# The first batch's steps in a fixed order, without T·B·K, merges by pairs of heads, the first weight split beside the substitution

## The chip, the cores and the metric

The kernel runs on one core of a Trainium2 chip. The metric is device time in microseconds (us), the median over runs. The engines of a core work side by side, each through its own list of instructions in order: PE (TensorE, matmuls; weight loads are listed as PEld), DVE (VectorE), ACT (ScalarE), POOL (GpSimd) and SP (SyncE, which here only issues DMAs). TensorE's clock has two levels, 1.2 and 2.4 GHz, which the profile gives as a granted share of 0.5 or 1.

## The reference

Two blocks: a delta-rule recurrence per head, then a Fourier mix with an MLP.

```python
B, H, S, D = 4, 8, 768, 48
k_n = k / (norm(k) + 1e-6);  state = zeros(B, H, D, D)
for t in range(S):
    y[:, :, t] = q_t @ state                       # before the update
    v_old = state.T @ k_t
    state += b_t * outer(k_t, v_t - v_old)
x = y.transpose(0, 2, 1, 3).reshape(B, S, 384)
u = x + real(fft(fft(x, axis=1), axis=2))
un = (u - mean(u)) / sqrt(var(u) + 1e-6)           # over the last axis
out = u + relu(un @ w_ch1) @ w_ch2                 # 384 -> 1536 -> 384
```

The two weights arrive as float64 and are turned into float32 on the chip, by integer work on their two 32-bit words.

## The kernel before, in words

**Chunks and quads.** The recurrence is worked in chunks of 64 tokens: 12 per batch, 48 in all, m = 0 to 47. Four chunks are a *quad* (three per batch, Q = 0 to 11), two quads a *group* g. For each quad `prepare` (L337) transposes keys and queries (`pt`, into KQT), takes their products (`pg`) and copies them out: key by key into A (L400 on DVE, L402 on ACT), query by key, masked, into LQ (L405, DVE). In the first batch keys and queries are prepared apart.

**Inverse.** Each chunk and head needs the inverse T of a 64x64 triangular matrix. `invert` (L428) turns the gram matrices so that each lane of DVE holds one (transpose L441), takes the key norms from the diagonal (`sm`), and does 30 steps of substitution (L465, L467) for blocks of 32x32, then turns the result back into Z and A (L483, L484). Groups 0 and 1 are inverted together. `merge` (L489) joins two 32-blocks to one 64-block by two rounds of small products (`pj`) and writes the table `wt`. A *round* is one of these two, for one quad.

**The chain.** `chain(m)` (L541) has three pieces, each the end of a `yield`: U = V − K·state (`pc<-st,KQT`, DVE L572); then for batches 1 to 3 U = T·U by `wt` (`pc<-U,wt`, ACT L584); then state += K·U (`pc<-U,kp`, DVE L600). In the first batch `combined` (L521) instead multiplies T into keys (`pm`) and values (`pv`) two chunks ahead, with two ACT copies, so that the chain itself is without the second piece. `outputs` (L610) forms y for two chunks (`py`), by an ACT copy (L635) and a DVE addition (L640, L642) into the x tiles.

**Second block.** `fourier(b)` (L668) mixes batch b (adds on DVE and POOL, products `pf` and `pb`), then means and variances; `mlp` (L755) takes three groups of 256 rows (`ph` with the first weight, `po` with the second). `weights(0)` converts w_ch1 (two ACT instructions L302, L304 and three DVE instructions L321, L324, L327 for a piece of 384 columns, 12 pieces), `weights(1)` w_ch2.

**What sets the order.** The body (L870 on) writes instructions as generators advance: in each piece of a chain step, `due` grows by PRE for preparation, inversion and merge of the next group and by SIDE for the second block of the batch before. The Tile framework then orders the instructions of each engine by its own planning, except where `keep_in_program_order` binds one. Batch 0 runs beside w_ch1's conversion; `second(0)` runs beside batch 1, and so on; the last batch's second block comes after all chains.

Of the kernel before, what the change touches and what calls it, by code (L numbers as in the profile page):

```python
# [10 lines left out]
F32 = mybir.dt.float32  # L11
# [6 lines left out]
CH = 64  # L18
W = 32
# [63 lines left out]
def kernel(  # L83
# [56 lines left out]
    nc.vector.memset(k0[:, D:], 0.0)  # L140
# [11 lines left out]
    kps = [zeroed([128, QT, 4, 64], f"kp{i}", nc.vector, pads) for i in range(NB)]  # L152
    qps = [zeroed([128, QT, 4, 64], f"qp{i}", nc.vector, pads) for i in range(1)]
# [61 lines left out]
    half_p = const.tile([NBH, 1], F32, name="half_p")  # L215
    nc.gpsimd.memset(half_p, 0.5)
    half_n = const.tile([128, GT], F32, name="half_n")
    nc.gpsimd.memset(half_n, -0.5)
    root = const.tile([NBH, 1], F32, name="root")
    nc.scalar.activation(root, half_p, ACT.Sqrt)  # L220

    bblk = const.tile([128, B * NQ * QT * 4], F32, name="bblk")

    def betas():
# [8 lines left out]
        nc.vector.tensor_copy(bcol.rearrange("p (b i) (c u) -> p b (i c) u", b=B, u=4),  # L233
# [4 lines left out]
        nc.vector.tensor_scalar(twice, twice, once, None, op0=ALU.mult)  # L238
        nc.vector.transpose(bblk, bcol.rearrange("p q n -> p (q n)"))
# [23 lines left out]
    def weights(part):  # L263

        if moe_w_ch1.dtype == F32:
            if part == 0:
                nc.sync.dma_start(out=w1, in_=moe_w_ch1.rearrange("(c p) f -> p c f", p=128))
            else:  # L270
                yield
                nc.sync.dma_start(out=w2, in_=moe_w_ch2.rearrange("(c p) m -> p c m", p=128))
            return
        w1v = moe_w_ch1.bitcast(I32).rearrange("(c p) (f two) -> p c f two", p=128, two=2)
        w2v = moe_w_ch2.bitcast(I32).rearrange("(c p) (m two) -> p c m two", p=128, two=2)
        nw = DFF // 2
        np_ = nw // 2
        if part == 0:
            halves = [(w1v[:, i, a * nw:a * nw + nw], w1[:, i, a * nw:a * nw + nw])
                      for i in range(KD) for a in range(2)]  # L280
            n, stage = 2, wk.tile([128, 2, nw, 2], I32, tag="hT", name="w64")
            stages = [stage[:, i] for i in range(2)]
        else:
            halves = [(w2v[:, i, a * np_:a * np_ + np_], w2[:, i, a * np_:a * np_ + np_])
                      for i in range(KF) for a in range(DM // np_)]
            n, stages = 1, [xpairs[6].rearrange("p t (f two) -> p (t f) two", two=2).bitcast(I32)]

        def fetched(i):
            if i < len(halves):
                nc.sync.dma_start(out=stages[i % 2], in_=halves[i][0])  # L290

        def words(p):
            t, cs = stages[p // n % 2], slice(p % n * np_, (p % n + 1) * np_)
            return t[:, cs, 0], t[:, cs, 1], tmps[:, p % 2]

        def first(p):

            lo, hi, t = words(p)
            tc.keep_in_program_order(nc.scalar.activation(  # L302
                t[:, 0], lo.bitcast(mybir.dt.uint32), ACT.Copy, scale=2.0 ** -29))
            tc.keep_in_program_order(nc.scalar.activation(  # L304
                t[:, 1].bitcast(F32), hi.bitcast(F32), ACT.Abs, scale=2.0 ** -112))

        for i in range(len(stages)):
            fetched(i)
        yield
        if part == 1:  # L310
            stages.append(wk.tile([128, np_, 2], I32, tag="scr", name="w64"))
            fetched(1)
        tmps = wk.tile([128, 2, 2, np_], I32, tag="F", name="wtmp")
        first(0)
        for p in range(n * len(halves)):
            lo, hi, t = words(p)
            dst = halves[p // n][1][:, p % n * np_:(p % n + 1) * np_].bitcast(I32)
            low, mag = t[:, 0], t[:, 1]
            if p + 1 < n * len(halves):
                first(p + 1)  # L320
            tc.keep_in_program_order(nc.vector.scalar_tensor_tensor(  # L321
                low, hi, -2 ** 31, low, op0=ALU.bitwise_and, op1=ALU.bitwise_or))
            yield
            tc.keep_in_program_order(nc.vector.tensor_scalar(  # L324
                mag, mag, 3, None, op0=ALU.logical_shift_left))
            u16 = mybir.dt.uint16
            nc.vector._custom_dve(dve_ops.ADD32_U16LIMBS, out=dst.bitcast(u16),  # L327
                                  in0=mag.bitcast(u16), in1=low.bitcast(u16))
            if (p + 1) % n == 0:
                fetched(p // n + 2)  # L330
            yield
# [3 lines left out]
    grams = {}  # L335

    def prepare(Q, parts=(0, 1)):  # L337
# [6 lines left out]
        if 0 in parts:  # L344
            if lh == 0:

                if g == 1:
                    grams[g] = w2.rearrange("p c m -> p (c m)")[:, 0:2 * QT * 4 * 2 * W].rearrange(
                        "p (c u l s) -> p c u l s", c=2 * QT, u=4, l=2)
                else:  # L350
                    grams[g] = wk.tile([128, 2 * QT, 4, 2, W], F32, tag="A", name="A")
# [6 lines left out]
        for c2 in range(QT // 2):  # L358
            for c in (2 * c2, 2 * c2 + 1):
# [8 lines left out]
                if QT * i + c < NCH // 2 or 1 not in parts:  # L368
                    nc.scalar.activation(dst, src, ACT.Copy)  # L369
                else:  # L370

                    if na == 2:
                        nc.scalar.activation(dst[:, 0], src[:, 0], ACT.Copy)
                    nc.scalar.activation(dst[:, na - 1], src[:, na - 1, :, ::-1], ACT.Copy)
# [568 lines left out]
```

## Time and profile before

| | us |
|---|---|
| median of 3 runs (806.78 to 818.7) | 809.28 |
| the profiled execution | 807.02 |
| its span, first to last instruction | 805.3 |
| busy in the span: PE / DVE / ACT / POOL | 691.7 / 382.3 / 263.0 / 55.5 |

The profiled execution is 1.7 us longer than its span. Busy time says how much of the span an engine was at work; in which stretch and behind which wait it stood still has to be read from the views below. "x16" beside a matmul counts instructions: a product of two float32 tiles is two of them, so eight products stand as x16.

### The profile page before, as it was taken

To read this page: it belongs to the slowest core of one execution; us is meant where nothing else is said; L and a number is where in the kernel's file an instruction comes from. 1 tells how busy PE (TensorE), PEld (TensorE's weight loads), DVE (VectorE), ACT (ScalarE), POOL (GpSimd) and SP (SyncE) were. 2 spreads that over 40 slices of the span, in tenths; PEclk is the share of its full clock that TensorE was granted. 3 is DMA by queue.
4 is the path that set the end of the run, shared out by engine and by line. 5 is a ranking of instruction groups with operands and counts; after the bars stand their busy time and mean duration, and the time that the engine had idled before them with its cause. 6 is when DMAs were issued, how large, how long until landed. Compare 5 with 4: busy or idle time off the path is not lost.

```text
span 805.3 us, 19785 instructions
## 1 busy us (share of the span) xinstructions
PE 691.7 (86%) x8600; PEld 513.8 (64%) x8600; DVE 382.3 (47%) x968; ACT 263.0 (33%) x622; POOL 55.5 (7%) x73
## 2 busy tenths in 40 slices
PE   5810798866999989689999999899999989999997
PEld 4600686665757757577575775676767657587684
DVE  3899536577991166835792113986111135200000
ACT  3400775621627422273123443223311122021120
POOL 5020000010000010001100000210000010000000
PEclk9999999867899995799999999899999999999999
DMA  6620046330431121101201100101000000000000
GB/s 107 179 55 0 2 117 140 66 57 25 137 94 32 21 50 37 31 8 23 43 16 25 41 13 12 31 2 30 13 11 11 11 11 1 11 11 20 11 10 21
DMA packets 82232, 30.89 MB, mean 38 GB/s; under 512 B 77296, under 2 KB 78832, under 8 KB 82144
## 3 DMA queue, kind: packets, MB, share of 16 engines
q1 hardware_dynamic: 78800, 26.24, 14.5%
q0 software_dynamic: 1168, 2.98, 1.2%
q8 instruction: 68, 1.11, 0.6%
q10 hardware_dynamic: 2176, 0.39, 0.3%
q14 instruction: 20, 0.16, 0.1%
HBM read 24.87 MB, written 4.72 MB: 37 GB/s over the span
## 4 chain that ended last, share of the span: by engine, by line
PE 64%; DVE 19%; ACT 7%; DMA 4%; issue 3%; SPq 2%; POOL 1%; POOLq 0%; ACTq 0%; DVEq 0%
PE ph L124 20%; PE po L124 19%; PE pc L124 5%; DVE A L465 4%; PE pg L124 3%; PE pf L124 3%; PE pj L124 3%; PE py L124 3%; PE pt L127 3%; ACT A L402 2%; DVE w L467 2%; DVE X L467 2%; DMA w<-in_moe_w_ch_dram 2%; PE pb L124 2%; SPq L169 2%
## 5 line engine op out<-in xcount | busy, mean ns | idle before, releaser
L124 PE MATMUL ph<-unT,w 128*128 128x256 f32 x864 | 213.2, 395 | 3.9 <-ACT hT L781 2.4
L124 PE MATMUL po<-w,hT 128*128 128x384 f32 x576 | 200.4, 495 | 0.9 <-ACT hT L781 0.4
L124 PEld LDWEIGHTS ph<-unT,w 128*128 128x128 f32 x864 | 160.5, 194 | 32.2 <-ACT hT L781 5.4
L124 PEld LDWEIGHTS po<-w,hT 128*128 128x128 f32 x576 | 104.9, 190 | 66.6 <-ACT hT L781 1.0
L781 ACT ACTIVATE hT<-ph 128x256 f32<-128x256 f32 x144 | 55.1, 384 | 179.2 <-PE ph L124 179.0
L794 DVE TENSOR_TENSOR x<-x,po 128x384 f32<-128x384 f32 x24 | 13.2, 549 | 103.5 <-PE po L124 103.5
L124 PE MATMUL pj<-Z,A 32*32 32x32 f32 x640 | 13.2, 201 | 45.5 <-DVE Z L483 45.2
L600 DVE TENSOR_TENSOR st<-st,pc 128x192 f32<-128x192 f32 x44 | 15.5, 351 | 68.5 <-PE pc L124 54.1
L465 DVE TENSOR_TENSOR A<-X 128x30 f32<-128x30 f32 (+14 forms) x120 | 42.8, 357 | 2.3
L402 ACT ACTIVATE A<-pg 32x256 f32<-32x256 f32 x104 | 35.7, 371 | 23.9 <-PE pg L124 23.3
L124 PE MATMUL pg<-KQT 48*64 48x64 f32 (+1 forms) x1024 | 38.8, 297 | 5.3 <-ACT KQT L369 4.5
L124 PEld LDWEIGHTS pj<-Z,A 32*32 32x32 f32 x640 | 12.2, 116 | 48.6 <-issue 43.6
L467 DVE TENSOR_TENSOR X<-X,A 128x30 f32<-128x30 f32 (+14 forms) x120 | 40.5, 337 | 2.3
L124 PE MATMUL pf<-stab,scr 128*128 128x128 f32 (+6 forms) x192 | 30.9, 310 | 12.1 <-DVE scr L692 11.9
L124 PEld LDWEIGHTS pg<-KQT 48*64 48x64 f32 x1024 | 31.0, 172 | 15.5 <-ACT KQT L369 6.9
L124 PE MATMUL py<-st,KQT 48*64 48x48 f32 x768 | 32.7, 246 | 8.3 <-DVE x L642 7.4
L572 DVE TENSOR_TENSOR U<-V,pc 128x192 f32<-128x192 f32 x48 | 16.8, 350 | 47.8 <-PE pc L124 46.2
L584 ACT ACTIVATE U<-pc 128x192 f32<-128x192 f32 x36 | 12.0, 332 | 83.5 <-PE pc L124 64.2
L661 POOL DMA_INDIRECT out_dram<-x,rows_hi x12 | 12.4, 1033 | 364.1 <-DVE x L794 174.6
L124 PEld LDWEIGHTS pf<-stab,scr 128*128 128x128 f32 (+2 forms) x192 | 26.9, 198 | 16.3 <-issue 7.3
L405 DVE TENSOR_TENSOR LQ<-pg,pack 128x512 f32<-128x512 f32 x24 | 16.4, 683 | 43.2 <-ACT A L402 39.4
L718 DVE TENSOR_TENSOR x<-x,pb 128x193 f32<-128x193 f32 (+1 forms) x96 | 26.4, 347 | 18.8 <-PE pb L124 18.8
(137 smaller groups left out, 908.8 us busy)
## 6 DMA issues: line engine op xcount, KB each, us to landing
qp<-in_q_dram SPq DMA_DIRECT2D x96, 48.0 KB, 2.4
V<-in_v_dram SPq DMA_DIRECT2D x96, 48.0 KB, 2.5
w<-in_moe_w_ch_dram SPq DMA_DIRECT2D x6, 768.0 KB, 6.0
kp<-in_k_dram SPq DMA_DIRECT2D x80, 48.0 KB, 2.5
x<-in_moe_w_ch_dram SPq DMA_DIRECT2D x6, 384.0 KB, 3.1
w<-in_moe_w_ch_dram SPq DMA_DIRECT2D x6, 384.0 KB, 3.4
out_dram<-x SPq DMA_DIRECT2D x8, 192.0 KB, 1.9
out_dram<-x SPq DMA_DIRECT2D x4, 168.0 KB, 2.1
```

What stands on the lines that cost most here:

```text
L124: return nc.tensor.matmul(o, lhsT=lhsT, rhs=rhs, start=start, stop=stop, skip_group_check=True)
L127: nc.tensor.matmul(o, lhsT=src, rhs=ident[0:src.shape[0], 0:src.shape[0]], is_transpose=True, start=start, stop=True, skip_group_check=True)
L169: engs[hh].dma_start(out=dst[64 * hh:64 * hh + CH, c, :, 0:D], in_=src[b, 4 * hh:4 * hh + 4, t0:t0 + CH, :].rearrange("h p d -> p h d"))
L402: nc.scalar.activation(ce(A[pr, ns, :, sl]), src, ACT.Copy)
L405: nc.vector.tensor_tensor(ce(LQ[:, 2 * c2:2 * c2 + 2]), pv[:, :, :, 1 - a0], mb[:, None, None, :].broadcast_to([128, 2, 4, CH]), op=ALU.mult)
L465: nc.vector.tensor_tensor(t, X[:, :, j:j + 1, j + 1:].broadcast_to([128, G, j, n]), X[:, :, 0:j, j:j + 1].broadcast_to([128, G, j, n]), op ...
L467: nc.vector.tensor_tensor(X[:, :, 0:j, j + 1:], X[:, :, 0:j, j + 1:], t, op=ALU.add)
L572: nc.vector.tensor_tensor(U.rearrange(ue, e=2), V4[:, c].rearrange(ue, e=2), pk, op=ALU.subtract)
L600: nc.vector.tensor_tensor(nst, st, pS, op=ALU.add)
L718: nc.vector.tensor_tensor(dst, dst, src, op=op)
L781: nc.scalar.activation(hT[:, fc, :], ph, ACT.Relu)
L794: nc.vector.tensor_tensor(x[g][:, tt, :], x[g][:, tt, :], po, op=ALU.add)
```

## The change

1. The first batch's chain gets the second piece too (T·U by `wt`); `combined` goes.
2. `merge` takes the 32-blocks of two heads at once: 64x64 products of which the two diagonal blocks are kept, half as many matmuls; the copies out are four of half the size instead of two. A is stored with its two copies apart, `[2, chunk, head, s]`.
3. Gram copies: two over 128 lanes and two over 32, instead of six over 32; in the first batch on ACT for the first half of a quad and on DVE for the second. The first batch's LQ is copied by ACT without its mask, and DVE masks it in SBUF later.
4. All four first quads' queries are prepared during the substitution (two before). w_ch1 is fetched in ten pieces of 384 KB from POOL's queue and split in place by ACT during the substitution; DVE joins it during the first batch.
5. From the end of the first substitution to the end of the first batch every DVE, ACT and PE instruction keeps program order, with a table that says what goes beside which piece of a step. Only quad 0 is merged before the chain starts; the second group's last transposes, the merges of quads 1 to 3 and the join go between the steps.
6. Preparation of group 2 (quads 4 and 5) starts with the second batch (PRE 4.6 there), not in the middle of the first. SIDE is 0, 1.5, 2.2, 2.2 for batches 0 to 3 (2.4 before).

```diff
+    class Ordered:
...
+        def __getattr__(self, name):
+            def call(*args, **kwargs):
+                ins = getattr(self.engine, name)(*args, **kwargs)
+                if strict[0]:
+                    tc.keep_in_program_order(ins)
+                return ins
+            return call
+
+    dve, act, pe = Ordered(nc.vector), Ordered(nc.scalar), Ordered(nc.tensor)
...
+    class FirstWeight:
+        def fetch(self, p, eng=nc.sync):
+            if p < self.n:
+                i, a = divmod(p, DFF // PW)
+                eng.dma_start(out=self.stage(p), in_=moe_w_ch1.bitcast(I32).rearrange(
+                    "(c p) (f two) -> p c f two", p=128, two=2)[:, i, PW * a:PW * a + PW])
+        def split(self, p):
+            if p < self.n:
+                lo, hi = words(self.stage(p))
+                digits(self.stage(p), lo, hi)
+        def join(self):
+            t = wk.tile([128, 2, PW], I32, tag="scr", name="wtmp")
+            for p in range(self.n):
...
+                for k, op in enumerate(joined(w1[:, i, PW * a:PW * a + PW], lo, hi, t[:, 0], t[:, 1])):
+                    op()
...
+                    yield
...
+    class Merge:
+        def products(self, step, half):
+            A, Z = self.A, self.Z
+            if half == 0:
+                self.pj = ps_pair("pj", "pair")
+            for c in (2 * half, 2 * half + 1):
+                n = QT * self.lh + c
+                for us in (slice(0, 2), slice(2, 4)):
+                    for hh in range(2):
+                        r1, r2 = slice(64 * hh, 64 * hh + W), slice(64 * hh + W, 64 * hh + 64)
+                        ops = (A[r2, 1, n, us], Z[r2, n, us]) if step == 0 else (A[r1, 0, n, us], A[r1, 1, n, us])
+                        o = 128 * c + W * us.start
+                        mm(self.pj[64 * hh:64 * hh + 64, hh, o:o + 64],
+                           *(a.rearrange("p u t -> p (u t)") for a in ops), c == 0 and us.start == 0)
...
     def chain(m):
...
-        if m < NCH:
-            if m + 2 < NCH:
-                combined(m + 2)
-        else:
-            pu = pc[:, 0, 4 * D:8 * D].rearrange("p (u d) -> p u d", u=4)
...
+        pu = pc[:, 0, 4 * D:8 * D].rearrange("p (u d) -> p u d", u=4)
...
+        act.activation(U, pu, ACT.Copy)
+        yield
...
-    PRE, SIDE = 2.4, (2.4, 2.4, 2.4, 2.4)
...
+    between = queries(0, 1, 2, 3)
+    for i in range(W - 2):
+        advance(first)
+        advance(between)
+        if i < 10:
+            w.fetch(i, nc.gpsimd)
+        if 10 <= i < 20:
+            w.split(i - 10)
...
+    strict[0] = True
+    M = Merge(0, 0)
...
+    scaled(0)
+    run(masks(0))
+    scaled(1)
+    run(masks(1))
+    pe_work = {m: (outs, outs, outs) if m % 2 == 0 else (outs, None, None) for m in range(2, NCH)}
+    for m, l, step in ((0, 1, 0), (1, 1, 1), (3, 2, 0), (5, 2, 1), (7, 3, 0), (9, 3, 1)):
+        pe_work[m] = (outs if m > 1 else None, P(l, step, 0), P(l, step, 1))
+    act_work = {0: [T(1, 0)], 1: [T(1, 1)], 2: [Dg(1)], 4: [T(2, 0), Dg(2)], 6: [T(2, 1)], 8: [T(3, 0), Dg(3)], 10: [T(3, 1)]}
+    rest = seq(w.join(), masks(3))
+    for m in range(NCH):
...
+        for i, _ in enumerate(chain(m)):
+            if pe_work[m][i]:
+                pe_work[m][i]()
+            if i == 1:
...
+                    advance(*((first, 1) if m < 3 else (rest, 4)))
+            if i == 2:
+                advance(rest, 1)
+                for op in act_work.get(m, ()):
+                    op()
...
+    strict[0] = False
+    PRE, SIDE = 2.4, (0.0, 1.5, 2.2, 2.2)
+    pre, side, due = ahead(2), iter(()), [0.0, 0.0]
+    for m in range(NCH, STEPS):
...
+                due[0] += 4.6 if g == 1 else PRE
+                due[1] += SIDE[b]
```

What the change moves is seen in the order of instructions on an engine. All instructions that go through the new wrapper carry its line, L131.

**PE, the first two steps of the chain** (`pc` are the chain's products, `pv` and `pm` those of T·V and T·K, `pj` merges). Before:

```order
L124 MATMUL pc<-st_89,KQT 64x48 x8
L124 MATMUL pm<-wt_83,kp_73 64x64 x4
L124 MATMUL pv<-V_318,wt_83 64x48 x6
L124 MATMUL pc<-U,kp_73 64x48 x8
L124 MATMUL pv<-V_318,wt_83 64x48
L124 MATMUL pj<-w_128 32x32 x32
L124 MATMUL pc<-st_90,KQT 64x48 x8
```

Changed:

```order
L131 MATMUL pc<-st_89,KQT 64x48 x8
L131 MATMUL pc<-U,wt_83 64x48 x8
L131 MATMUL pj<-Z,A 64x64 x8
L131 MATMUL pc<-U,kp_73 64x48 x8
L131 MATMUL pj<-Z,A 64x64 x8
L131 MATMUL pc<-st_90,KQT 64x48 x8
```

`pm` and `pv` are gone, `pc<-U,wt` stands in the chain, and a merge of 32 products has become two halves of 8.

**DVE, a step of the first batch** (U and st are the chain's two results; SCALAR_TENSOR_TENSOR, TENSOR_SCALAR and ISA on w and wtmp join w_ch1; x is the output addition). Before:

```order
L572 TENSOR_TENSOR U<-V_318,pc 128x2x2x48
L321 SCALAR_TENSOR_TENSOR wtmp<-w_453,wtmp 128x384
L327 ISA w_127<-wtmp 128x768
L600 TENSOR_TENSOR st_89<-st_91,pc 128x192
L321 SCALAR_TENSOR_TENSOR wtmp<-w_453,wtmp 128x384
L572 TENSOR_TENSOR U<-V_318,pc 128x2x2x48
```

Changed:

```order
L131 TENSOR_TENSOR U<-V_310,pc 128x2x2x48
L131 TENSOR_TENSOR x_145<-x_145,py 128x384
L131 SCALAR_TENSOR_TENSOR wtmp<-w_446 128x384
L131 TENSOR_SCALAR wtmp<-w_446 128x384
L131 ISA w_127<-wtmp 128x768
L131 SCALAR_TENSOR_TENSOR wtmp<-w_446 128x384
L131 TENSOR_TENSOR st_90<-st_89,pc 128x192
```

Four join instructions, and in odd steps an output addition ahead of them, now stand between U and st.

**DVE, the end of the first batch** (X<-A opens the inversion of group 2; scr<-x opens the Fourier mix of batch 0; un<-x opens the MLP). Before:

```order
L600 TENSOR_TENSOR st_91<-st_90,pc 128x192
L572 TENSOR_TENSOR U<-V_1364,pc 128x2x2x48
L441 STREAM_TRANSPOSE X<-A 128x1024
L405 TENSOR_TENSOR LQ<-pg,pack 128x2x4x64
L642 TENSOR_TENSOR x_146<-x_146,py 128x384
L561 COPY st_89<-p_2029 128x192
L682 TENSOR_TENSOR scr<-x_146 128x384
```

Changed, some 65 rows behind the first scr<-x and 20 behind the first un<-x:

```order
L131 TENSOR_TENSOR LQ<-pg,pack 128x2x4x64
L131 TENSOR_TENSOR st_90<-st_89,pc 128x192
L131 TENSOR_TENSOR LQ<-pg,pack 128x2x4x64 x2
L131 STREAM_TRANSPOSE X<-A 128x1024
L131 SCALAR_TENSOR_TENSOR wtmp<-wtmp 128x384
```

The inversion of group 2, which stood ahead of the Fourier mix, now stands behind it, among the joins of w_ch2.

## Rows read from the trace of the kernel before

**Rows 1.** Stretches: us; busy PE, PEld, DVE, ACT, POOL; clock; DMA share; GB/s.

```profile
0.00:84.70 84.70, 30.31 (x480) 22.55 (x480) 67.17 (x138) 17.29 (x44) 15.46 (x25) 1.00 0.36 81
98.30:124.50 26.20, 26.19 (x686) 23.27 (x686) 11.28 (x28) 18.92 (x42) 0.00 (x0) 1.00 0.42 102
201.40:242.80 41.40, 38.67 (x270) 27.67 (x270) 38.84 (x102) 19.18 (x44) 1.51 (x2) 0.94 0.38 113
302.50:336.70 34.20, 28.32 (x415) 22.43 (x408) 23.64 (x67) 7.39 (x19) 2.37 (x3) 0.56 0.19 36
```

**Rows 2.** Timeline, DVE, up to the first step: start, us, engine, line, instruction.

```profile
41.31 0.96 DVE L198 TENSOR_TENSOR V<-V,ln 128x768 f32<-128x768 f32 x1 [0.18 <-DMA qp<-in_q_dram]
...
45.78 0.68 DVE L405 TENSOR_TENSOR LQ<-pg,pack 128x512 f32<-128x512 f32 x1
...
80.44 2.36 DVE L476 TENSOR_TENSOR Y<-Y,w 128x1024 f32<-128x1024 f32 x2
82.71 1.97 DVE L483 STREAM_TRANSPOSE Z<-Y 128x1024 f32<-128x1024 f32 x1
...
98.35 0.35 DVE L572 TENSOR_TENSOR U<-V,pc 128x192 f32<-128x192 f32 x1 [1.19 <-PE pm L124]
```

**Rows 3.** Timeline, the chain's products and copies at three places.

```profile
98.76 0.71 PE L124 MATMUL pc<-U,kp 64*64 64x48 f32 x16
...
231.90 0.67 PE L124 MATMUL pc<-U,wt 64*64 64x48 f32 x16
...
235.27 0.45 PE L124 MATMUL pc<-U,kp 64*64 64x48 f32 x16
...
314.23 0.69 PE L124 MATMUL pc<-st,KQT 48*64 48x48 f32 x16
...
315.57 0.55 DVE L642 TENSOR_TENSOR x<-x,py 128x384 f32<-128x384 f32 x1
315.68 1.09 PE L124 MATMUL pc<-U,wt 64*64 64x48 f32 x16
...
316.86 0.33 ACT L584 ACTIVATE U<-pc 128x192 f32<-128x192 f32 x1 [0.59 <-PE pc L124]
```

**Rows 4.** Timeline, DVE, from the last step of the first batch.

```profile
160.32 0.35 DVE L572 TENSOR_TENSOR U<-V,pc 128x192 f32<-128x192 f32 x1 [0.84 <-PE pc L124]
161.94 1.90 DVE L441 STREAM_TRANSPOSE X<-A 128x1024 f32<-128x1024 f32 x1 [1.26 <-ACT A L402]
...
239.10 1.98 DVE L483 STREAM_TRANSPOSE Z<-Y 128x1024 f32<-128x1024 f32 x1
```

**Rows 5.** Timeline, DVE, around the start of the third batch.

```profile
323.80 0.35 DVE L572 TENSOR_TENSOR U<-V,pc 128x192 f32<-128x192 f32 x1 [0.42 <-PE pc L124]
...
356.62 0.35 DVE L572 TENSOR_TENSOR U<-V,pc 128x192 f32<-128x192 f32 x1 [1.83 <-PE pc L124]
```

**Rows 6.** Timeline, PE: products of 64x64 at four places of the array, and a merge round.

```profile
124.83 0.46 PE L124 MATMUL pm<-wt,kp 64*64 64x64 f32 x16
...
241.13 1.20 PE L124 MATMUL pj<-Z,A 32*32 32x32 f32 x64 [1.10 <-DVE Z L483]
```

**Rows 7.** Stretch 166 to 300, instructions of `pt`: busy PE, PEld, ACT.

```profile
166.00:300.00 134.00, 5.02 (x32) 4.02 (x32) 4.91 (x10) 0.90 0.24 59
```

**Rows 8.** Stretch 161.9 to 190, instructions on tile X (the inversion): busy DVE.

```profile
161.90:190.00 28.10, 7.42 (x16) 0.64 0.24 44
```

**Rows 9.** The same stretch, instructions on `sm` (the norms): busy DVE, ACT, POOL.

```profile
161.90:190.00 28.10, 5.00 (x15) 0.23 (x1) 2.25 (x1) 0.64 0.24 44
```

**Rows 10.** Groups by line: busy us, mean ns, then idle before and its releasers.

```profile
L124 PE MATMUL ph<-unT,w 128*128 128x256 f32 x864 | 213.2, 395 | 3.9 <-ACT hT L781 2.4 <-ACT unT L769 0.6 <-ACT gz L715 0.5
L302 ACT ACTIVATE wtmp<-w 128x384 int32<-128x384 uint32 x18 | 10.0, 554 | 8.5 <-DMA w<-in_moe_w_ch_dram 5.7 <-DVE w L327 1.4 <-DMA kp<-in_k_dram 0.9
```

**Rows 11.** DMA issues: KB each, us to landing; and a timeline row of SP's queue.

```profile
w<-in_moe_w_ch_dram SPq DMA_DIRECT2D x6, 384.0 KB, 3.4
...
19.38 5.93 SPq L169 DMA_DIRECT2D V<-in_v_dram  x8
```

More of the change, by code (lines that the diff above doesn't have):

```diff
@@ L273, in weights, with second_weight @@
+    def second_weight():
+        if moe_w_ch1.dtype == F32:
+            yield
+            nc.sync.dma_start(out=w2, in_=moe_w_ch2.rearrange("(c p) m -> p c m", p=128))
             return
-        w1v = moe_w_ch1.bitcast(I32).rearrange("(c p) (f two) -> p c f two", p=128, two=2)
         w2v = moe_w_ch2.bitcast(I32).rearrange("(c p) (m two) -> p c m two", p=128, two=2)
[L276 to L305, printed above, removed]
@@ L307, in weights @@
-        for i in range(len(stages)):
-            fetched(i)
-        yield
[L310 to L322, printed above, removed]
-            yield
[L324 to L330, printed above, removed]
+        stages = [xpairs[6].rearrange("p t (f two) -> p (t f) two", two=2).bitcast(I32)]
@@ L588, in chain @@
             loads()
-            if Q + 1 < len(quads):
+            if Q + 1 < len(quads) and Q + 1 not in vals:
                 values(Q + 1)
@@ L647, in advancing @@
             gens.pop(0)
-        yield
     def store(b, T, x):
@@ L814, in seq, with kept @@
             yield from gen
+    def kept(gen):
+        while True:
+            strict[0] = True
+            more = advance(gen)
+            strict[0] = False
+            if not more:
+                return
+            yield
     def ahead(g):
@@ L875 @@
     run(keys(2, 3))
-    side = weights(0)
-    advance(side)
+    values(1)
+    w = FirstWeight()
     tables()
     first = invert(0, 1)
-    advance(first, 5)
-    between = queries(0, 1)
+    advance(first, 4)
+    between = queries(0, 1, 2, 3)
[6 more added lines that the diff above has]
+            w.split(i - 10)
+    run(between)
     while not isinstance(grams[0], tuple):
@@ L883 @@
         advance(first)
-        advance(between)
-    run(between, both(merge(0, (0,)), merge(0, (1,), "py")))
-    combined(0)
-    combined(1)
-    pre = seq(first, merge(1), queries(2, 3))
-    due = [0.0, 0.0]
-    for m in range(STEPS):
+    strict[0] = True
+    M = Merge(0, 0)
+    for step in range(2):
+        M.products(step, 0)
+        M.products(step, 1)
+        M.taken(step)
+        M.diagonal(step)
+    scaled(0)
+    run(masks(0))
+    scaled(1)
+    run(masks(1))
+    outs = lambda: advancing(later)
```

357 lines of the change are left out of this document (207 added, 150 removed).

## The prediction

> **What bounds the kernel now.** I read the stretches first, then the timeline of DVE at their borders, then the groups. Four regimes are to be seen.
>
> Up to 84.7 the substitution holds DVE (67.2 busy of 84.7) while PE works 30.3 [rows 1]; this head ends with the first U of the chain at 98.35 [rows 2].
>
> The first batch runs from that U to the one of step 11 at 160.32 [rows 4]: 62.0 for 11 steps, 5.6 each. PE is full up to 124.5 (26.2 of 26.2) [rows 1]. The clock column prints 1.00 for the first of these stretches, but the same eight products take 0.71 at 98.76 and 0.45 at 235.27 [rows 3], and 0.69 in a stretch of mean clock 0.56 [rows 1, 3]. So I take PE to be at 1.2 GHz until about 124.
>
> The passage to the second batch runs until Z of group 2 is turned at 239.10 [rows 4]. DVE is the limit there: Fourier mix, inversion and w_ch2; in its second part DVE is busy 38.8 of 41.4 [rows 1].
>
> From there on PE bounds, with one hole: between 302.5 and 336.7 it is busy 28.3 of 34.2 at mean clock 0.56 [rows 1], and step 24's U at 323.80 is followed by step 25's only at 356.62 [rows 5]. By the counts in the body, 51 advances of the MLP at 2.4 a piece are used up after 21 pieces, in step 19; steps 20 to 23 run without any, and step 24 waits for its inversion.
>
> **The change, term by term**, against the profiled execution (807.0; the median is 2.3 higher).
>
> *Head.* From DVE's path before the first Z go four LQ masks and two scalings of V (0.6 and 0.9 from start to start, from rows of 0.68 and 0.96) and the second half of the Y product (1.1): 5.3 [rows 2]. I take 5.0, since the square root's round trip loses some cover. Then, in fixed order on DVE, come the second transpose (1.8, a start-to-start like Z's 1.97), the two scalings and four masks (4.2), then what opens the chain: two small products with v0, p0 and its copy (2.5, estimated from the 0.35 and 0.7 of like instructions [rows 3]) and the first products to U (0.9): 9.4 from Z's end. Z ended at 84.7, so the new U stands at 79.7 + 9.4 = 89.1, against 98.35: −9. Merging quad 0 (two rounds on PE, 12 ACT copies) fits into these 9.4. The extra queries, the fetches and the splits cost nothing as long as they hide under the substitution, where ACT and POOL are busy 17.3 and 15.5 of 84.7 [rows 1]. The splits are 20 x 0.55 = 11 [rows 10]. Five of them stand ahead of the square root in ACT's order and wait for their 384 KB, 3.4 to land [rows 11]; if the transfers come one behind the other, that is 17 after the first issue at about 12, still before the root at 37. Bounds −4 to −12.
>
> *First batch.* A step is now three pieces in line. At 1.2 GHz: 0.69 + 1.09 + 0.71 of products (the middle one uses two places of the array and is slower), 0.35 + 0.33 + 0.35 of copies, and 0.5 for six handovers: 4.0; eleven are 44. Beside that: in the odd steps 3 to 9 the output addition (0.55, itself behind an ACT copy) and four join instructions stand between U and st, and half a merge delays a piece: 0.9 each, 3.6. Steps 0 and 1 carry halves of a merge: 1.0. Eight ACT copies in a row at steps 4 and 8 hold up U's: 1.4. Quad 2's values can only be fetched once step 3 has let go of the buffer, and eight issues take 5.9 [rows 11] for a use three steps later: 1. Sum 51, against 62.0: −11. The products of T·K and T·V lie beside the old chain, so their going is inside this difference. Lower bound of the new time: at 2.4 GHz a step is 0.45 + 0.67 + 0.45 + 1.5 = 3.1 [rows 3], in all 40; upper: no gain, 62.
>
> *Passage.* What was done beside the Fourier mix now lies behind it: of the inversion 7.4 on X and 5.0 on the norms, less 2.1 counted in both [rows 8, 9], and four LQ masks (2.4): 13 on DVE. The preparation of quads 4 and 5 costs PE 5.0 for its transposes alone, by two later quads [rows 7]; it falls where PE has room. So Z of group 2 comes at 239.1 − 9 − 11 + 13 = 232. While DVE is at it, PE gets further: by the order of the changed kernel 15 of the 36 `ph` products of the second row group are ahead of group 2's merge, 30 instructions of 213.2/864 = 0.247 [rows 10], −7. The passage gives back +13 − 7 = +6; bounds 0 (the inversion fills the gaps of w_ch2 as it did those of the mix) and +20 (DVE's new work is exposed, waits between its small operations included, and nothing gets ahead on PE).
>
> *Merges.* A round is 64 instructions in 1.20 [rows 6], after it 32. Products of the width of 64 take, for 32, from 0.75 (two rows like the `pm` one at four places [rows 6]) to 1.2 (two like `pc<-U,wt`, which uses the same two places as the new merges [rows 3]). I take the near one, 1.1: for the 16 rounds behind the passage −2, bounds −7 and +1.
> The Trainium skill ("TensorE: Matmul & The Clock Gate", "Wait — 56ns, not 53.3ns?") says that starts of matmuls never come closer than about 25 ns however small they are. By that half the instructions would be near half the time, 0.8 a round, and the term −6; the trace has 19 ns from one to the next (1.20/64), so it does not agree, and the weights' place decides.
>
> *Hole at the third batch.* At 1.5 a piece, 51 advances last 34 pieces, up to step 23. So PE has MLP work through steps 16 to 23, quads 6 and 7 are prepared with less in front of them, and their inversion starts earlier against step 24. The hole is worth 34.2 − 28.3 x 0.56 = 18 [rows 1]; I take 13 of it, bounds 0 and 18.
>
> Gram copies in four instead of six and the smaller copies of the merges lie on ACT beside PE: 0.
>
> Sum: −9 − 11 + 6 − 2 − 13 = −29: **778**.
>
> **Rivals.** *(a) PE's clock rises in the first batch.* With eight products at 0.45 in place of 0.7 a step is 3.1 and the batch 40: −11 more, **767**. For it: the new chain keeps PE some 80% busy. Against it: 26 us of full PE with small products stayed at 0.71 [rows 1, 3]. Chance 0.15. The Trainium skill (the same page, "What's actually happening") says that the throttled clock is the default and that activity releases it; by that rule this would be the likely case, and the trace, where a full PE stayed slow, does not agree.
>
> *(b) The passage keeps what the first batch gives.* DVE stays full, all 13 go behind the mix, PE finds no work ahead (the `po` products wait for w_ch2), and step 24 goes on waiting for its inversion, so that the hole stays: −9 − 11 + 13 − 2 = −9, **798**. For it: DVE 38.8 of 41.4 [rows 1], and the inversion's place in the order. Chance 0.2.
>
> *(c) Slower: PE falls to 1.2 GHz in the second batch.* With 1.5 in place of 2.4 advances the chain's small products make up more of PE's stream. Place: from Z of group 2 to step 24, about 90. It decides when the granted clock there is 0.56, as in the hole, instead of about 1. Each busy us then costs up to 1.8: half the stretch at that rate is +36, on −29 + 13 (the hole gives nothing): 827. Against it: the stretch 201.4 to 242.8, with the MLP beside the chain, has 0.94 [rows 1]. Beyond about 16 of such loss it is slower than before. Chance 0.06.
>
> *(d) The order isn't kept.* The changed order shows DVE, ACT and PE as the table says, so I give that no chance of its own.
>
> **Numbers.** The forecast has 0.59, (a) 0.15, (b) 0.2, (c) 0.06. The likeliest case gives 778; its own range is 764 to 792, the two terms with the widest bounds (passage and hole) each half way out. With (a) and most of (b): 756 to 800. A change under 2% (16) is about what a measurement of this kernel can't tell from none. Faster by over 2% is below 793: nearly all of the forecast, all of (a), a quarter of (b): 0.78. Within 2%: the rest of (b), a little of the forecast and of (c): 0.17. Slower 0.05.
>
> **What would show it.** The first U near 89, and Z of group 0 near 78 to 80; eleven steps in 50 to 53, with eight products at 0.7 up to the Fourier mix (0.45 there is rival a); Z of group 2 near 232, with `ph` running from about 180; a merge round near 1.1; steps 20 to 24 about as long as 16 to 19, with no low clock there. Wrong would be: DVE waiting for values or PE for `py` inside a step, the square root late behind the splits, or a passage of over 95 from step 11 to Z.

## The result and the profile after

The changed kernel takes **786.5 us** (786.3 to 786.6) against 809.3 of the kernel before on the same chip: ratio 0.970, 95% interval 0.9635 to 0.977. A second timing, on another chip, gave 0.967 (0.963 to 0.971). The forecast was 778, range 756 to 800: the time lies inside the range, 8 above the likeliest case. The profiled execution takes 786.5 with a span of 784.7, against 807.0 and 805.3, so the spans differ by 20.6 where the sum of the terms was 29.

Stretches of the changed kernel: us; busy PE, PEld, DVE, ACT, POOL; clock; DMA share; GB/s.

```profile
0.00:79.00 79.00, 42.56 (x624) 29.68 (x624) 53.75 (x112) 33.23 (x80) 20.63 (x35) 1.00 0.56 123
89.10:140.30 51.20, 47.08 (x1036) 41.17 (x1040) 33.55 (x71) 23.47 (x56) 0.00 (x0) 1.00 0.29 60
...
174.40:193.10 18.70, 17.25 (x245) 13.60 (x245) 9.02 (x21) 14.78 (x41) 1.53 (x2) 0.92 0.55 125
193.10:236.90 43.80, 39.92 (x171) 27.25 (x171) 40.84 (x114) 16.82 (x39) 2.65 (x2) 0.96 0.32 78
236.90:301.90 65.00, 58.96 (x947) 41.32 (x946) 40.15 (x103) 24.89 (x64) 2.13 (x2) 0.95 0.15 29
301.90:333.60 31.70, 26.62 (x347) 21.61 (x347) 14.43 (x30) 19.02 (x47) 1.73 (x3) 0.73 0.11 24
...
301.90:311.00 9.10, 5.11 (x94) 3.96 (x94) 7.78 (x12) 5.56 (x13) 0.83 (x2) 0.98 0.19 44
311.00:328.00 17.00, 16.26 (x181) 13.29 (x181) 2.06 (x7) 9.88 (x24) 0.90 (x2) 0.51 0.08 14
```

They answer to [rows 1]: head, first batch, then the two halves of the passage that lie behind the Fourier mix, the second batch, and the stretch that was called the hole, with two pieces of it. Note the third: TensorE is nearly full there while DVE has half its time free. The timeline of DVE at the borders (start, us, engine, line, instruction):

```profile
78.57 2.02 DVE L131 STREAM_TRANSPOSE Z<-Y 128x1024 f32<-128x1024 f32 x1
...
89.07 0.35 DVE L131 TENSOR_TENSOR U<-V,pc 128x192 f32<-128x192 f32 x1 [0.91 <-PE pc L131]
...
140.31 0.35 DVE L131 TENSOR_TENSOR U<-V,pc 128x192 f32<-128x192 f32 x1
...
174.39 0.45 DVE L131 TENSOR_SCALAR un<-x,mv,rstd 128x384 f32<-128x384 f32 x1
...
193.11 1.96 DVE L131 STREAM_TRANSPOSE X<-A 128x1024 f32<-128x1024 f32 x1
...
236.92 2.07 DVE L131 STREAM_TRANSPOSE Z<-Y 128x1024 f32<-128x1024 f32 x1
...
301.91 0.35 DVE L131 TENSOR_TENSOR U<-V,pc 128x192 f32<-128x192 f32 x1
...
333.62 0.35 DVE L131 TENSOR_TENSOR U<-V,pc 128x192 f32<-128x192 f32 x1
```

In order: Z of group 0, the first U, step 11, the first `un` (the mix is over), the inversion of group 2 starts, its Z, step 24, step 25. The counterparts are in [rows 2, 4, 5]. And the chain's products on PE, with a merge round:

```profile
88.32 0.68 PE L131 MATMUL pc<-st,KQT 48*64 48x48 f32 x16
...
150.55 5.07 PE L131 MATMUL pf<-stab,scr 128*128 128x65 f32 x24 [0.16 <-DVE scr L131]
155.55 0.68 PE L131 MATMUL pc<-st,KQT 48*64 48x48 f32 x16
...
158.02 0.45 PE L131 MATMUL pc<-U,kp 64*64 64x48 f32 x16 [0.25 <-ACT U L131]
...
239.05 1.15 PE L131 MATMUL pj<-Z,A 32*64 32x64 f32 x32 [1.06 <-DVE Z L131]
```

Eight products take 0.68 all through the first batch and up to 155.55; behind the mix's first `pf` products they take 0.45. The 1.00 of the clock column for the first batch is no measurement: the profile has no record of the clock before 157.

### The profile page after: what moved, and what is told of

Its sections match the earlier page's. It is cut to its first block, busy times and chain, and to the rows that moved or that the text cites. A ratio compares the mean times of both kernels' runs of the same rounds, so it can differ in the third digit from the quotient of the medians.

```text
span 784.7 us, 17842 instructions
## 1 busy us (share of the span) xinstructions
PE 699.9 (89%) x7640; PEld 513.0 (65%) x7640; DVE 379.4 (48%) x952; ACT 260.0 (33%) x634; POOL 58.7 (7%) x83
## 4 chain that ended last, share of the span: by engine, by line
PE 48%; DVE 10%; ACT 5%; issue 3%; DMA 0%; SPq 0%; POOL 0%; POOLq 0%; DVEq 0%; ACTq 0%
PE ph L131 20%; PE po L131 15%; DVE X L131 3%; PE pc L131 3%; DVE A L131 2%; PE pf L131 2%; PE pj L131 2%; ACT A L131 2%; PE pb L131 2%; ACT wt L131 1%; PE pg L131 1%; PE py L131 1%; DVE sm L131 1%; DVE x L131 1%; PE pt L131 1%
## 5 line engine op out<-in xcount | busy, mean ns | idle before, releaser
L131 PE MATMUL ph<-unT,w 128*128 128x256 f32 x864 | 213.8, 395 | 4.5 <-ACT unT L131 2.0
L131 PE MATMUL po<-w,hT 128*128 128x384 f32 x576 | 202.2, 498 | 1.7 <-ACT KQT L131 0.7
L131 PEld LDWEIGHTS ph<-unT,w 128*128 128x128 f32 x864 | 160.3, 193 | 33.7 <-ACT hT L131 3.7
L131 PEld LDWEIGHTS po<-w,hT 128*128 128x128 f32 x576 | 105.7, 191 | 68.2 <-issue 1.5
L131 ACT ACTIVATE hT<-ph 128x256 f32<-128x256 f32 x144 | 54.9, 383 | 179.6 <-PE ph L131 179.3
L131 DVE TENSOR_TENSOR x<-x,po 128x384 f32<-128x384 f32 x24 | 13.2, 552 | 112.5 <-PE po L131 112.4
L131 ACT ACTIVATE U<-pc 128x192 f32<-128x192 f32 x48 | 15.9, 331 | 110.0 <-PE pc L131 98.4
L131 ACT ACTIVATE KQT<-pt 128x256 f32<-128x256 f32 (+1 forms) x82 | 32.0, 419 | 44.9 <-PE pt L131 44.3
L131 PEld LDWEIGHTS pc<-U,wt 64*64 64x64 f32 x768 | 34.0, 163 | 19.7 <-issue 10.3
L131 PE MATMUL pg<-KQT 48*64 48x64 f32 (+1 forms) x1024 | 41.7, 309 | 5.5 <-ACT KQT L131 4.4
L131 PEld LDWEIGHTS pg<-KQT 48*64 48x64 f32 x1024 | 32.1, 178 | 20.4 <-ACT KQT L131 11.2
L131 PE MATMUL pc<-U,wt 64*64 64x48 f32 x768 | 41.2, 253 | 4.7 <-DVE U L131 2.1
L131 DVE TENSOR_TENSOR st<-st,pc 128x192 f32<-128x192 f32 x44 | 15.3, 347 | 61.0 <-PE pc L131 56.8
L131 DVE TENSOR_TENSOR U<-V,pc 128x192 f32<-128x192 f32 x48 | 16.8, 350 | 53.1 <-PE pc L131 52.9
L131 DVE TENSOR_TENSOR A<-X 128x30 f32<-128x30 f32 (+14 forms) x120 | 41.0, 342 | 2.9
L131 DVE TENSOR_TENSOR X<-X,A 128x30 f32<-128x30 f32 (+14 forms) x120 | 39.5, 329 | 2.9
L131 DVE TENSOR_TENSOR x<-x,pb 128x193 f32<-128x193 f32 (+1 forms) x96 | 26.4, 346 | 23.1 <-PE pb L131 23.1
L131 PE MATMUL pt<-pack,kp 128*128 128x128 f32 x96 | 24.4, 349 | 10.3 <-DMA pack<-k_pack 4.8
L131 PE MATMUL pt<-pack,qp 128*128 128x128 f32 x96 | 23.4, 341 | 11.0 <-DMA qp<-in_q_dram 11.0
L131 PE MATMUL pj<-Z,A 32*64 32x64 f32 x320 | 15.0, 257 | 19.9 <-DVE Z L131 19.6
L131 ACT ACTIVATE A<-pg 128x256 f32<-128x256 f32 (+1 forms) x72 | 25.4, 378 | 21.7 <-PE pg L131 16.6
```

Source lines behind the costliest of these rows:

```text
L131: ins = getattr(self.engine, name)(*args, **kwargs)
```

## The experiments

Every kernel is the changed one with the edit shown. Ratios are to the kernel before on the same chip; the changed kernel itself has 0.970 and 0.967.

**The number of MLP advances** (step: the hole).

```
-    PRE, SIDE = 2.4, (0.0, 1.5, 2.2, 2.2)
+    PRE, SIDE = 2.4, (0.0, 2.4, 2.4, 2.4)
```

The edit sets the later batches back too, from 2.2 to 2.4; that bears on step 24 and what follows.

> The changed kernel with 2.4 instead of 1.5 MLP advances a piece in the second batch (and 2.4 for 2.2 later). If the slower feeding is what closed part of the hole at the third batch, as the prediction had it (13 of 18), the time goes from 786.5 to about 800, with step 24 to step 25 longer than 31.7 and a longer spell of low clock. If step 24 waits for the inversion and the merging of its own quads whatever the MLP does (Z of group 3 came at 306.0, four us behind that step's U, and four merge rounds behind it), the time stays within 783 to 790 and the stretch from step 24 to 25 within 2 of 31.7.

800.1, ratio 0.9895 (0.9865 to 0.993): the number is worth about 2% of the time, as the first theory said, and the profiled spans differ by 11.8 (796.5 against 784.7). Its stretches (columns as above):

```profile
290.00:311.00 21.00, 20.52 (x354) 15.69 (x358) 13.78 (x38) 5.00 (x13) 1.13 (x1) 0.53 0.18 37
311.00:328.00 17.00, 11.42 (x85) 9.58 (x78) 14.62 (x41) 4.11 (x11) 1.60 (x2) 0.67 0.19 34
328.00:346.90 18.90, 16.13 (x245) 13.43 (x246) 4.75 (x8) 14.17 (x31) 0.00 (x0) 0.82 0.03 6
```

And the kernel before the change, from the start of the hole to step 24:

```profile
302.50:323.80 21.30, 20.93 (x373) 15.96 (x367) 13.59 (x38) 5.00 (x13) 0.77 (x1) 0.53 0.18 37
```

With 2.4 TensorE is full at half its clock for 21 us before the third batch, as it was before the change; with 1.5 the clock is up until 311. But step 24 to 25 only falls from 35.8 to 31.7. Of the 11.8, 2.9 come before Z of group 2, 6.3 between it and step 24, 4.1 in step 24, and 1.5 are given back behind it.

**The free order** (step: head and first batch).

```
-    strict[0] = True
     M = Merge(0, 0)
```

> The changed kernel with the first batch's instructions free for the scheduler to reorder, everything else alike. If the fixed order is worth something beside the shorter chain, the 51.2 from step 0 to step 11 go up to 54 to 60 and the time to 790 to 796. If the shorter chain (three pieces, no products of T with K and V) does it all, they stay within 1.5 of 51.2 and the time is 785 to 788.

806.1, ratio 0.997 (0.994 to 1.001): without the fixed order nearly the whole gain is gone. It doesn't go where either theory put it. Step 0's U can't serve as the start here: it stands at 66.31, inside the substitution. From step 1 to step 11 it takes 47.4 (116.41 to 163.81) against 46.3. The gain goes in the head. DVE's groups from 40 to 101.8 in this kernel (busy us, mean ns, idle before):

```profile
L131 DVE CUSTOM_DVE_ANT_0 w<-wtmp 128x768 uint16<-128x768 uint16 x12 | 6.8, 563 | 0.0
L131 DVE SCALAR_TENSOR_TENSOR wtmp<-w 128x384 int32<-128x384 int32 x8 | 4.5, 561 | 0.0
...
L131 DVE TENSOR_TENSOR LQ<-LQ,pack 128x512 f32<-128x512 f32 x6 | 4.2, 699 | 2.0 <-ACT LQ L131 2.0
L131 DVE TENSOR_SCALAR wtmp<-w 128x384 int32<-128x384 int32 x8 | 2.9, 362 | 0.0
...
L131 DVE SCALAR_TENSOR_TENSOR wtmp<-x 128x384 int32<-128x384 int32 x4 | 2.2, 562 | 0.0
...
L131 DVE TENSOR_TENSOR V<-V,ln 128x768 f32<-128x768 f32 x2 | 1.9, 954 | 0.2 <-DVE sm L131 0.2
L131 DVE TENSOR_SCALAR wtmp<-x 128x384 int32<-128x384 int32 x4 | 1.5, 364 | 0.0
```

Twelve joins of the first weight (17.9), six masks and two scalings, 24.0 together, now stand inside the substitution, and DVE is busy 54.8 of these 61.8. So Z of group 0 comes at 101.78 instead of 78.57, 23.2 later. The order is mainly a fence that keeps work which has time out of the head. In the steps it is worth less: with no join left in them they take 47.4 here, and 44.9 in the next run, which has no joins either but keeps the order.

**The joins** (step: the odd steps' 0.9). The three join instructions are left out and the weight is a constant.

```
-                    op()
                     if k == 1 and p + len(self.stages) < self.n:
```

> The changed kernel without the joining of w_ch1 on DVE (36 groups of three instructions less beside the first batch; the weight is a constant instead, so the output differs). The odd steps 1, 3, 5, 7 and 9 take 4.9, 4.9, 5.8, 4.9 and 5.8 against 4.0 of the even ones. If the joins between U and the next state hold them up, as one half of the prediction's reason had it, they fall by 0.3 to 0.9 each and the eleven steps to 47 to 49.5. If the half merges on TensorE do, they stay: 50.5 to 51.5.

787.8 in a single run, too few to compare; its output differs. Steps 1, 3 and 7 stay at 4.87, 4.88 and 4.87; steps 5 and 9 fall from 5.8 to 5.12 each; the eleven steps take 49.8, between what the two theories gave. In steps 1, 3 and 7 the joins cost nothing, and step 1, which has half a merge on TensorE and no output addition yet, is as long as the others: that points to the half merge for the 0.9. The joins cost 0.7 in each of two steps.

**Quads 4 and 5 prepared inside the first batch** (step: passage).

```
+            if m in (6, 8):
+                advance(prep[4])
+            if m in (10, 11):
+                advance(prep[5])
...
-        for Q in (2 * g, 2 * g + 1):
+        for Q in (2 * g, 2 * g + 1) if g != 2 else ():
```

> The changed kernel with quads 4 and 5 prepared inside the first batch (behind the pieces of steps 6, 8, 10 and 11) instead of behind the Fourier mix. In the changed kernel the mix ends at 174.4 and the inversion of group 2 starts at 193.1; between them PE is busy 17.2 of 18.6 and DVE 8.9. If this preparation on the path is what made the passage 5 longer than predicted, that 18.7 falls under 5; the first batch, where PE is 92% busy, gets longer by 10 (if its clock rises with the 128-wide transposes) to 20 (if not): 778 to 789, with Z of group 2 before 232 in the first case. If the passage is bound by DVE's total and not by that preparation, Z of group 2 stays at 237 or comes later by the 10 to 20 of the first batch: 790 to 805.

792.2, ratio 0.971 (0.964 to 0.979): no difference. DVE's timeline in that kernel:

```profile
117.32 0.35 DVE L131 TENSOR_TENSOR U<-V,pc 128x192 f32<-128x192 f32 x1 [0.33 <-PE pc L131]
...
126.85 0.69 DVE L131 TENSOR_TENSOR LQ<-pg,pack 128x512 f32<-128x512 f32 x1 [4.04 <-ACT A L131]
127.46 0.34 DVE L131 TENSOR_TENSOR U<-V,pc 128x192 f32<-128x192 f32 x1
...
158.05 0.34 DVE L131 TENSOR_TENSOR U<-V,pc 128x192 f32<-128x192 f32 x1
...
164.93 1.94 DVE L131 STREAM_TRANSPOSE X<-A 128x1024 f32<-128x1024 f32 x1
...
236.60 2.07 DVE L131 STREAM_TRANSPOSE Z<-Y 128x1024 f32<-128x1024 f32 x1
...
315.73 0.35 DVE L131 TENSOR_TENSOR U<-V,pc 128x192 f32<-128x192 f32 x1 [3.13 <-PE pc L131]
335.75 0.35 DVE L131 TENSOR_TENSOR U<-V,pc 128x192 f32<-128x192 f32 x1 [0.65 <-PE pc L131]
```

From step 11 to Z it takes 78.6, as before the change (78.8, [rows 4]) and 18.1 less than in the changed kernel (96.6). The first batch takes 69.3 instead of 51.2, 18.0 more. The inversion moved with its preparation: it starts at 164.93, beside the mix, which ends at 196.87. So the two together make up the passage's growth, and they cost 18 in either place; this run doesn't price the one without the other. TensorE stays at the low clock through this batch (eight products 0.68 at 151.69). Part of the 18 is this kernel's own placing: a mask of LQ waits 4.04 for ACT's copies, and step 7's U stands behind it on DVE (step 6 takes 10.1 instead of 4.0). A placing with the mask a step later wasn't tried. Step 24 no longer waits there: Z of group 3 comes at 300.34, 15 ahead of its U, and it takes 20.0 to step 25 instead of 31.7. But from Z of group 2 to step 24 it takes 79.1 instead of 65.0, so the shorter step 24 gained nothing in all.

**The same with TensorE's order left free.**

```
-                if strict[0]:
+                if strict[0] and not (pe_free[0] and self is pe):
                     tc.keep_in_program_order(ins)
```

> The kernel that prepares quads 4 and 5 inside the first batch, with TensorE's order there left to the scheduler (DVE and ACT keep the table's order). That kernel had 69.3 for the eleven steps against 62.0 of the kernel before, which also prepared quads 4 and 5 there and whose clock rose at 124. If the fixed order on TensorE is what makes the preparation cost its full 18 there (its pieces stand in front of the chain's), the free order packs it into waits: 56 to 63 for the eleven steps and 774 to 781 at the speed of the first chip. If TensorE is simply full at the low clock, it stays at 66 to 71 and 785 to 790.

790.0, ratio 0.976 (0.969 to 0.983); the eleven steps take 69.6. TensorE's order isn't what costs the 18; that leaves its clock, low for most of the batch, and the order on DVE and ACT, which this run doesn't tell apart.

**Group 2's inversion not held until the mix is over.**

```
-        while g == 2 and 0 not in mixed:
-            yield
```

> The changed kernel without the rule that group 2's inversion waits for the end of the first Fourier mix. If the place behind the mix costs the passage what the prediction put down for it (13 on DVE, 7 given back on PE), Z of group 2 comes some 10 before 236.9, the mix ends later than 174.4, and the time is 778 to 783. If DVE's whole work up to Z is the same in either order, Z stays within 3 of 236.9, the MLP starts later and the ph products that ran ahead of the merge are lost: 790 to 794.

785.9, ratio 0.973 (0.967 to 0.980). The inversion starts at 193.46 and Z comes at 235.90, both as in the changed kernel: the rule isn't what holds it. The preparation does, which stands behind the mix in program order: the inversion reads the A that it writes. Neither theory's premise was met.

**Merging head by head.**

```
-                for us in (slice(0, 2), slice(2, 4)):
+                for u in range(4):
...
-                        mm(self.pj[64 * hh:64 * hh + 64, hh, o:o + 64],
+                        mm(self.pj[r1, hh, o:o + W], *ops, c == 0 and u == 0)
```

> The changed kernel with merging head by head again: 64 instead of 32 instruction records a round, 32x32 outputs, ACT copies of whole rows (2 instead of 4 a round). The prediction had 0.1 to 0.15 a round for the pairs, 2 in all: 788.5. By the trace of the changed kernel a round of pairs takes 1.15 at full clock against 1.20, so nothing is expected of PE; with half as many copies on ACT behind each round, the wait between two rounds (1.5 of copies at 309.9) gets shorter: 784 to 787, with step 24 to 25 shorter by 1 to 2.

786.8, ratio 0.972 (0.970 to 0.975). A round there, on PE, and the copies behind it, on ACT:

```profile
238.27 1.20 PE L131 MATMUL pj<-Z,A 32*32 32x32 f32 x64 [1.07 <-DVE Z L131]
...
240.17 1.19 ACT L131 ACTIVATE A<-pj 32x512 f32<-32x512 f32 x2
```

Half the instructions save 0.05 a round, and the copies behind a round of pairs are dearer (1.53 in four against 1.19 in two). Step 24 to 25 takes 26.1 here instead of 31.7, which work behind it takes back. The term was 2; it is nothing.

**A warm TensorE** (rival a). Products with unused results beside the last 20 steps of the substitution; in the second kernel also one behind each piece of the chain.

```
+        if i >= 10:
+            dve.memset(mark[:, i:i + 1], 0.0)
+            warm(64, mark[:, i:i + 1])
+            warm(256)
```

> The changed kernel with products on idle TensorE beside the substitution (for each of its last 20 steps one of 64 columns tied to that step and one of 128x128x256, results unused). Two theories on the first batch, whose eight products took 0.68 for 51 us with PE busy 47.1 of 51.2. If the low clock there is left over from the idle head, the eight products start at 0.45 with the clock already up and stay there: 40 to 44 for the eleven steps instead of 51.2, time 773 to 778. If the chain's small products can't hold the clock by themselves, it falls again in the first steps: 48 to 52 for the eleven steps and 784 to 789.

791.2 on a chip where the kernel before takes 814.5: 0.9725 (0.965 to 0.980). PE's timeline and the stretches:

```profile
74.49 0.70 PE L131 MATMUL pw<-stab,pack 128*128 128x256 f32 x2
80.69 1.97 PE L131 MATMUL pj<-Z,A 32*64 32x64 f32 x32 [5.50 <-DVE Z L131]
```

```profile
79.00:89.00 10.00, 5.99 (x88) 4.79 (x88) 8.73 (x11) 5.38 (x12) 0.00 (x0) 0.55 0.01 2
89.00:140.40 51.40, 47.11 (x1040) 41.17 (x1040) 33.57 (x72) 23.54 (x56) 0.00 (x0) 0.50 0.29 60
```

The clock is up until the idle 5.5 us before the first merge (the last unused product, 128x256, takes 0.70 at 74.49, like one of `ph` of that shape at 185.16 in the changed kernel); then the merge round takes 1.97 instead of 1.15, and the whole first batch runs at 0.50, 1.2 GHz, in the same 51.2 as before.

```
             if pe_work[m][i]:
                 pe_work[m][i]()
+            warm(128)
```

> As the run before, and one more product of 128x128x128 (result unused) behind each piece of each step in the first batch, 36 in all. If such products keep the clock up, a step's pieces take 0.45, 0.67 and 0.45 instead of 0.68, 1.09 and 0.68: the eleven steps 40 to 46, and the stretch up to the end of the mix gets shorter too, 765 to 778. If the clock stays low, each of them costs up to 0.5 in a queue that is 92% busy: 55 to 65 for the eleven steps, 790 to 803.

812.3, ratio 0.995 (0.990 to 0.999). The first batch takes 69.2, 18.0 more for 36 products: 0.5 each. One stretch of it:

```profile
89.00:158.00 69.00, 69.00 (x1098) 57.28 (x1102) 34.12 (x71) 23.62 (x55) 0.00 (x0) 0.50 0.22 46
```

TensorE has no idle time in 69 us and stays at 1.2 GHz. The Trainium skill ("TensorE: Matmul & The Clock Gate", "What's actually happening") says that activity releases the throttle; being busy with products like these did not release it, by this row.

**Two more numbers of the planner**, timed beside the changed kernel.

```
-                due[0] += 4.6 if g == 1 else PRE
+                due[0] += 4.6 if g in (1, 2) else PRE
```

> The changed kernel with 4.6 instead of 2.4 advances a piece for the preparation and inversion of group 3 in steps 16 to 23. If their pace in the program's order is what brings Z of group 3 (306.0) behind the U of step 24 (301.9), the inversion starts some 5 before 268.7, step 24 to step 25 falls from 31.7 to 26 to 29, and the time is 3 to 5 below the changed kernel's. If TensorE's total work up to step 24 decides, Z and U of step 24 move against each other and the time stays within 2 of it.

785.6 against 784.4: 0.968 (0.964 to 0.972) against 0.967. Group 3's inversion starts at 266.55 against 266.29 in the changed kernel beside it: its pace in the program doesn't set its start, and that theory fell.

> The changed kernel itself once more, as the measure for the two runs beside it: 0.970 of the kernel before, within the interval of its first timing (0.9635 to 0.9768).

784.4, 0.967 (0.963 to 0.971); its profiled span is 780.9, so between two profiles of one kernel a difference of 4 tells nothing.

```
-    PRE, SIDE = 2.4, (0.0, 1.5, 2.2, 2.2)
+    PRE, SIDE = 2.4, (0.0, 1.2, 2.2, 2.2)
```

> The changed kernel with 1.2 instead of 1.5 MLP advances a piece in the second batch, so that some 8 of the 51 are left for step 24. 2.4 to 1.5 gave 13. If what is gained comes from MLP work that keeps TensorE busy and its clock up where the chain waits for the inversion, the low spell from 311 to 328 gets shorter and the time is 2 to 6 below the changed kernel's. If the work left over only stands in front of step 24's merging and its own products, step 25 comes later and the time is 2 to 6 above it.

786.6, 0.969 (0.965 to 0.973): no difference. Step 24 comes 5 earlier (294.23 against 299.51), and step 25 2 later (333.42 against 331.05). Below 1.5 nothing more was gained. No kernel here beats the changed one.

## Why the prediction came out as it did

The kernel with 2.4 carries every part of the change but the number of MLP advances (2.4 also in the later batches), and so separates the terms. From landmark to landmark, in us of the profiles:

| | before | change with 2.4 | changed |
|---|---|---|---|
| to the first U | 98.35 | 89.04 | 89.07 |
| to step 11 | 61.97 | 51.24 | 51.24 |
| to Z of group 2 | 78.78 | 99.49 | 96.61 |
| to step 24 | 84.70 | 71.32 | 64.99 |
| to step 25 | 32.82 | 35.78 | 31.71 |
| to the end | 448.68 | 449.63 | 451.08 |

*Head, −9:* −9.3, right; by the run with free order it rests on the fence.

*First batch, −11:* −10.7. The step itself is right: the even steps 2, 4, 6, 8 and 10 take 3.92 to 4.07 against 4.0 by the sum of pieces. That the whole is right too is partly luck. What stands beside the pieces came to 7.2 against 7.0, but from other places: steps 5 and 9 took 0.9 more each than forecast (the joins are most of it), steps 0 and 1 together 0.8 more, while the 1.4 of ACT copies at steps 4 and 8 and the 1.0 of quad 2's values did not come (4.07 and 4.05; no wait in this batch is put down to a DMA). What the prediction didn't price is the preparation that left the batch: put back in, with that run's placing, it makes the batch 69.3, longer than the 62.0 of before. So no run shows that the new chain by itself gains anything. None puts the products of T·K and T·V back, or the old copies of the gram matrices and of LQ; what these parts are worth stays open.

*Passage, +13 on DVE:* **this is where the mechanism failed, though the time fell inside the range.** The passage grew by 20.7 at 2.4 and 17.8 at 1.5, and its 96.6 is past the 95 that the prediction had named as a sign of being wrong. The sentence that was wrong is that the preparation "falls where PE has room", so that it cost nothing. Between the end of the mix and the start of the inversion TensorE is busy 17.25 of 18.7, with DVE at 9.02. The instructions of `pt` and `pg`, the preparation, and of `ph`, the MLP, in that stretch (in this order; the first number behind the 18.70 is PE's busy time), and the last wait of DVE before the inversion:

```profile
174.40:193.10 18.70, 4.23 (x25) 2.90 (x24) 4.44 (x13) 0.92 0.55 125
174.40:193.10 18.70, 5.62 (x128) 4.23 (x128) 2.67 (x4) 5.64 (x16) 0.92 0.55 125
174.40:193.10 18.70, 5.61 (x22) 4.02 (x23) 1.15 (x3) 0.92 0.55 125
...
192.50 0.69 DVE L131 TENSOR_TENSOR LQ<-pg,pack 128x512 f32<-128x512 f32 x1 [3.36 <-ACT A L131]
```

The inversion reads the A that the preparation writes, so it can't start before it. The two halves of the passage, up to the end of the mix and behind it, in the kernel before and in the changed one (columns as in the first table of stretches):

```profile
160.32:201.42 41.10, 27.84 (x376) 23.20 (x368) 31.61 (x98) 7.79 (x19) 5.62 (x7) 0.73 0.22 42
201.42:239.10 37.68, 36.08 (x179) 25.78 (x180) 35.12 (x99) 17.52 (x41) 1.51 (x2) 0.93 0.42 124
...
140.31:174.39 34.08, 28.70 (x438) 23.99 (x430) 22.44 (x71) 8.59 (x18) 3.47 (x6) 0.95 0.26 60
174.39:236.92 62.53, 57.20 (x415) 40.87 (x415) 49.87 (x134) 31.61 (x80) 4.18 (x4) 0.95 0.39 92
```

Behind the mix DVE has 14.7 more work, near the 13 of the prediction. Two things were left out of it. The mix, with 9.2 less of DVE's work beside it, ends 7.0 sooner. And behind the mix DVE is idle 10.1 more (12.7 against 2.6); 9.7 of the 12.7 lie in the 18.7, where its three longest waits (2.8, 3.0 and 3.4) end with the preparation's copies on ACT. 14.7 + 10.1 − 7.0 = 17.8, so the two errors in part cancel. The run that moved preparation and inversion back has 78.6 again; an inversion behind the mix without the preparation in front of it was not tried.

*Credit on PE and merges, −7 and −2:* from Z to the end the change with 2.4 gains 9.5. By the run with single heads none of it is the merging. The MLP work done before Z can be counted: 114 `ph` instructions with 28.3 us of PE in the kernel with 2.4, 90 with 21.1 in the changed one, 72 with 17.5 before (30 more were forecast). But it isn't free, as the prediction had it: it shares TensorE with the preparation. With 2.4 the stretch from the mix's end to the inversion has 40 `ph` instructions instead of 22 and takes 26.4 instead of 18.7.

*Hole, −13:* −11.8 by profiles, 13.6 by the medians (on two chips), so the size was right. The place was only partly: 4.1 in step 24. Step 24 goes on waiting for its inversion. On DVE, PE and ACT there:

```profile
305.96 2.02 DVE L131 STREAM_TRANSPOSE Z<-Y 128x1024 f32<-128x1024 f32 x1
...
308.04 1.15 PE L131 MATMUL pj<-Z,A 32*64 32x64 f32 x32 [1.54 <-DVE Z L131]
...
309.94 1.53 ACT L131 ACTIVATE A<-pj 32x256 f32<-32x256 f32 x4
...
311.52 1.97 PE L131 MATMUL pj<-A 32*64 32x64 f32 x32 [2.34 <-ACT A L131]
```

Z comes 4 us behind the step's U, rounds and copies alternate, and in between the clock falls. The gain goes with the low spell, which starts near 290 with 2.4 and near 311 with 1.5. What sets the start of group 3's inversion stays open; its pace in the program does not.

The sum: −9.3 − 10.7 + 20.7 − 9.5 − 11.8 = −20.6. Against −29 the passage is 7.7 off and the number of advances 1.2; the rest cancels.

*Rivals.* (a) is false: 0.68 up to the mix, and neither kernel with unused products raised the clock in the first batch. (b) is half true: the passage takes the first batch's gain back and step 24 still waits, but DVE isn't full (72.3 of 96.6), TensorE does find work ahead, and the hole's term is there. (c) did not come: the stretch from Z to step 24 has a mean clock of 0.95.

## What to carry to other kernels

When work leaves a stretch, ask which engine it will hold where it lands and who waits for it there; "it falls where there is room" has to be read off that engine's row, and work that runs ahead there can be what takes the room. A fixed order pays where it keeps work that has time out of a stretch that has none; look for what a scheduler slips into the chain that bounds. A planner's number set back by itself shows its worth, and where in time that worth lies. And a sum that comes out right is no proof of its terms: add them up one by one against the profile.

## What the runs showed of the hardware

- TensorE without a gap for 69 us stayed at 0.50 of its clock with the chain's small products and single 128x128x128 ones between them. In the changed kernel the clock came up behind the mix's first run of `pf` (5.07 at 150.55). With TensorE's order free and quads 4 and 5 beside the chain, eight chain products took 0.45 at 113.17 and 114.96, and 0.68 again at 117.88.
- The clock column prints 1.00 before a profile's first record of the clock (157.1 in the changed kernel, 56.0 in the warmed one): the first batch reads 1.00 in the one and 0.50 in the other, with 0.68 for the same products in both.
- A merge round of 32 instruction records with 64 columns takes 1.15, one of 64 with 32 columns 1.20: half the instructions at twice the width saved 0.05.
- The weight's fetches of 384 KB issued from POOL's queue take 6.4 and 9.2 to land (medians, two kinds of buffer), those from SP's 3.2 and 3.7; other loads were under way, and how much of the difference is the queue wasn't tried.
